# Largest key by products of whole key rows, a maximum along the free axis, and another planned order

## The chip, the cores and the metric

The kernel runs on one core of one Trainium2 chip. The metric is the device time of one execution in microseconds (us). The core has five engines that work side by side: TensorE (PE, whose weight loads are shown apart as PEld), VectorE (DVE), ScalarE (ACT), GpSimd (POOL) and SyncE (SP), which issues most DMAs. Each takes its instructions in the order in which the program gives them to it, and waits where an operand isn't there yet.

## The reference

Two branches over 2048 tokens of 448 features, and a gate for each token that mixes them. Branch A is attention with 16 heads of 28; branch B is a filter in the frequency domain.

```python
B, S, D = 1, 2048, 448
H = 16; Dh = D // H
g = sigmoid((x * gate_w).sum(-1, keepdims=True))
qkv = (x @ wqkv).reshape(B, S, 3, H, Dh).transpose(2, 0, 3, 1, 4)
q, k, v = qkv[0], qkv[1], qkv[2]
p = softmax(einsum("bhqd,bhkd->bhqk", q, k) * Dh ** -0.5)
a = (einsum("bhqk,bhkd->bhqd", p, v)).transpose(0, 2, 1, 3).reshape(B, S, D) @ wo
X = rfft2(x.astype(float32)) * (w_r + 1j * w_i)
b = irfft2(X, s=(S, D)).astype(bfloat16)
return g * a + (1 - g) * b
```

## The kernel before

The 16 heads are worked in four groups of four; the four heads of a group lie at partitions 0, 32, 64 and 96, 28 features each and a few rows for corrections. The queries go in 16 chunks of 512 tokens (four for each group), the keys in 16 tiles of 128. A score tile is keys by queries of one head, 128x512, a PSUM bank; there are 1024. Each is turned into exponentials in one of two ways: ACT computes them (line 1267, mostly two tiles in one instruction), or DVE writes an integer version that read as bf16 is about a power of two (line 1291), and POOL adds two shifted copies of up to three such tiles at once (line 1099). A tile that ACT made needs one product with the values V, a tile by way of DVE three.

All matrix products are issued by the helper at line 395, so they share this line, and are told apart by their tiles. `mc` splits a product by its columns of weights into strips of 32, at four positions of the array, which can run at the same time.

Scores are shifted by the largest squared norm of a key of the head, so that the exponentials stay in range. For group 0 this is done in units `kw0` with code of its own. For groups 1 to 3, POOL squares each chunk of keys (`e_ks`, line 732, into a free part of oT), and the unit `kw1`, `kw2` or `kw3` (function `largest`) works in six steps: `e_kx_pe` multiplies 16 tiles of squared keys with a selector of four columns, so that tokens lie on partitions and 64 sums on the free axis; `e_kx_m1` takes the maximum over the 16 tiles (128x4); `e_kx_tr` turns that round with the identity (4x128); `e_kx_mm` takes the maximum over 128; `e_kx_bc` spreads the four numbers over the heads' rows; `e_kx_kc` moves them to kc, which is added when q is moved out of PSUM (line 710). The q units of a group wait for its kw unit. The selector and the spreading matrix are columns 521 to 652 of the constant cA, which one DMA (`cA2`) brings.

The order of everything is set at build time by a planner written in Python (`Planner`, `stream`). It keeps a model clock for each engine, with durations written beside each step (`cols(n)` for a product of n columns, `dve(n)`, `act(n)`, or a number in us), and at each step places the piece of work that it can start first, ranked by due times. A unit's due time is a share of T plus an offset from the table OFF; some fifty parameters in PAR steer the choice between ACT and DVE, how early a unit may be taken and how many banks are kept. The engines then run the planned order whatever the real durations are.

The first 20 us prepare: x is loaded and transposed (units X0 to X7), folded on POOL for branch B (`e_xf`, lines 836 and 838, four pairs, xr and xe), the weights are loaded and spread to strips of 32 (line 474: `pk0` and `pq0` for group 0 on POOL, `pq1` and `pk1` for the other groups on DVE), and group 0's q and k are computed. The first fold waits for `pq0`, which waits for the load `wq0`. Small memsets on POOL behind the first pair (line 456) release later loads: the constants cC1 and cA2, and the weights wq1 and wk1 of the other groups, issued on SP's queue in this order.

Of the kernel before, what the change touches and what calls it, by code (L numbers as in the profile page):

```python
# [10 lines left out]
F32 = mybir.dt.float32  # L11
# [16 lines left out]
def fft_consts():  # L28
# [83 lines left out]
    A = np.zeros((128, 128 + 128 + 128 + 128 + 13 + 128))  # L112
    A[:, 0:128] = np.eye(128)
    for h in range(4):
        r = 32 * h
        A[r:r + 28, 128 + r + 28] = -0.5
        A[r:r + 28, 256 + r + 29] = -0.5
        A[r + 29, 512 + h] = 1.0
        A[r + 28:r + 32, 517 + h] = 1.0
        A[r:r + 28, 521 + h] = 1.0  # L120
        A[h, 525 + r + 29] = -0.5 * ALPHA
# [98 lines left out]
class Planner:  # L220
# [26 lines left out]
    def place(self, t, start):  # L247
        t.start = start
        t.end = start + t.dur
        if t.eng == "PE":  # L250
            if t.strips is None:
                self.strip = [t.end] * 4
                self.issue = t.end
            else:
                self.run_strips(t.strips, start + (0.0 if t.mode == self.mode else SW), True)
                t.end = max(self.strip)
        t.done = t.end + t.land
        t.placed = True
        self.free[t.eng] = t.end
        if t.mode is not None:  # L260
            self.mode = t.mode
        self.order.append(t)
        if t.then is not None:
            t.then(t)
# [34 lines left out]
class Kernel:  # L299

    PAR = dict(T=368, margin=0, dve_lead=1, pool_lead=8.025, early=156.198, dmargin=0, join=0.35, veff=0.55, vnext=0, vnb=2, nfa=6, nfd=1, flush=0.5, hold=4, n_dve=320, late=15.112, fill=0, cp=1.494, slack=0, zgap=0.3, vurg=24.651, nfa2=5, nfd2=0, trk=0.4, vrk=2.7, fitm=0.024, ukeep=3, dkeep=0, k3=4, w3=0, w2=0.055, amax=2, ulate=4, dsolo=0, k21=0, a21=0.7, qdn=15)


    OFF = dict(X0=-7.48, X1=-31.15, X2=-8.76, X3=-7.73, X4=10.34, X5=-2.42, X6=-12.59, X7=-5.72, q0_0=6.23, k0_0=13.58, k0_0b=13.14, k0_1=10.39,
               k0_2=-7.69, k0_3=19.38, kw0=3.44, v0_0=-126.42, v0_1=-47.49, v0_2=-26.74, v0_3=-11.95, q0_1=-18.46, q0_2=-3.0, q0_3=-2.59, gate=40.63,
               F1_0=12.99, F1_1=-23.99, F1_2=-34.12, F1_3=15.2, F1_4=7.02, F1_5=-8.21, F1_6=-1.1, F1_7=0.68, F1_8=6.09, F1_9=-43.2, F1_10=-34.66,
               F1_11=5.95, F1_12=8.95, F1_13=-13.79, F1_14=-3.63, F1_15=-17.27, k1_0=-15.54, k1_1=-1.12, k1_2=-6.24, kw1=-36.06, q1_0=7.64,
               v1_0=49.1, v1_1=49.43, v1_2=34.42, v1_3=-2.89, q1_1=-1.83, q1_2=23.85, q1_3=4.34, F2_0=-50.65, F3_0=55.06, F5_0=45.8, F2_1=-58.49,
               F3_1=-4.19, F5_1=31.73, F2_2=26.6, F3_2=6.07, F5_2=30.52, F2_3=-46.89, F3_3=37.68, F5_3=21.32, F2_4=-56.28, F3_4=7.86, F5_4=-1.49,
               F2_5=-19.46, F3_5=1.17, F5_5=45.52, F2_6=4.84, F3_6=1.14, F5_6=20.28, F2_7=9.15, F3_7=-17.95, F5_7=34.2, F2_8=27.09, F3_8=23.63,  # L310
               F5_8=57.9, F2_9=11.01, F3_9=11.74, F5_9=40.11, F2_10=3.19, F3_10=-20.19, F5_10=55.54, F2_11=-37.06, F3_11=50.1, F5_11=-45.25,
               F2_12=1.51, F3_12=-5.91, F5_12=37.08, F2_13=2.29, F3_13=-26.01, F5_13=7.42, F2_14=43.5, F3_14=25.25, F5_14=3.35, F2_15=-2.43,
               F3_15=33.4, F5_15=31.47, k2_0=-5.71, k2_1=-33.99, k2_2=-1.53, q2_0=-0.05, v2_0=8.32, v2_2=29.56, v2_3=15.17, q2_1=34.06, k3_0=-6.1,
               k3_1=14.07, k3_2=12.31, k3_3=-0.05, kw3=-8.76, q3_0=-29.03, v3_0=-4.47, v3_1=16.17, v3_2=11.35, v3_3=13.22, q3_1=0.16, q2_2=-2.51,
               q3_2=-24.22, q2_3=33.9, q3_3=-34.58, rg0=-0.08, rg1=-58.47, rg2=-25.93, rg3=-11.88, F6_0=1.79, F6_1=17.88, F6_2=1.0, F6_3=11.06,
               F6_4=50.13, F6_5=17.68, F6_6=60.78, F6_7=89.16, F6_8=61.03, F6_9=-9.62, F6_10=51.89, F6_11=-11.36, F6_12=5.82, F6_13=-35.13,
               F6_14=4.87, F6_15=35.02, o_1=5.5, o_2=28.97, o_3=-2.53, o_4=62.4, o_5=22.28, o_6=49.87, o_7=2.15, o_8=11.15, o_10=-22.91, o_11=21.75,
               o_12=-15.4, o_13=-16.58, o_14=17.26, o_15=-19.09)
# [15 lines left out]
    def sb(self, name, shape, dt=BF16):  # L334
        return self.per.tile(shape, dt, name=name)


    def tiles(self):
# [17 lines left out]
        self.cA = sb("cA", [128, 653])  # L356
# [21 lines left out]
        self.mx = sb("mx", [128, 1])  # L378
        self.kc = [sb(f"kc{i}", [128, 1], F32) for i in range(2)]
# [37 lines left out]
    def head(self):  # L417
# [18 lines left out]
        load("wq0", rawv[:, :, 0:112], wv[:, :, 0:112], 2.9, "ACT")  # L436
# [23 lines left out]
        load("cA2", self.cA[:, 521:653], C["A"].ap()[:, 521:653], 2.5, deps=[gate["cC1"]])  # L460
# [45 lines left out]
    def make_units(self):  # L506
# [4 lines left out]
        def unit(name, target, phases, deps=(), **k):  # L511
            u = U[name] = Unit(name, target + self.OFF.get(name, 0.0), phases, deps, **k)
            self.P.units.append(u)
            return u
# [7 lines left out]
        for k in range(4):  # L522
            dep[f"xr{k}"] = self.P.add("POOL", 1.84, lambda k=k: self.e_xf(k, 0), deps=[dep[f"x{k}"], dep["xrz"], dep["pq0"]], key=-5 if k == 0 else 0.5 * k)
            dep[f"xe{k}"] = self.P.add("POOL", 1.84, lambda k=k: self.e_xf(k, 1), key=-4.9 if k == 0 else 0.5 * k + 0.1,
                                       deps=[dep[f"xr{k}"], U[f"X{2 * k}"], U[f"X{2 * k + 1}"]])
# [56 lines left out]
        def largest(g, t0):  # L582

            unit(f"kw{g}", t0, [("PE", 0.43, self.e_kx_pe, (g,), "col"), ("DVE", 0.2, self.e_kx_m1, (g,)),
                                ("PE", 0.06, self.e_kx_tr, (g,), "col"), ("DVE", 0.25, self.e_kx_mm, (g,)),
                                ("PE", 0.04, self.e_kx_bc, (g,), "col"), ("DVE", 0.12, self.e_kx_kc, (g,))],
                 [dep[f"ks{g}_{c}"] for c in range(4)] + [dep["cA2"], dep["mxz"]], rank=-1)
# [146 lines left out]
    def e_kx_pe(self, b, g):  # L734
        for i in range(16):
            self.mc(b[:, 4 * i:4 * i + 4], self.oT[:, 3, 128 * i:128 * i + 128], self.cA[:, 521:525])

    def e_kx_m1(self, b, g):
        self.nc.vector.tensor_reduce(out=self.m1[:], in_=b[:, 0:64].rearrange("p (i h) -> p h i", h=4), axis=AX.X, op=ALU.max)

    def e_kx_tr(self, b, g):
        self.mm(b[0:4, 128:256], self.m1[:], self.ident, pos=(0, 0))

    def e_kx_mm(self, b, g):
        self.nc.vector.tensor_reduce(out=self.mx[0:4, :], in_=b[0:4, 128:256], axis=AX.X, op=ALU.max)

    def e_kx_bc(self, b, g):
        self.mc(b[:, 256:257], self.cA[:, 525:653], self.mx[:])
# [898 lines left out]
```

## Time and profile before

| what | us |
|---|---|
| median of 3 runs | 373.57 |
| lowest and highest of them | 373.29, 377.33 |
| the profiled execution | 373.71 |
| its span, first to last instruction | 371.9 |
| TensorE busy | 361.9 |
| ScalarE busy | 353.2 |
| VectorE busy | 325.6 |
| GpSimd busy | 320.1 |

A busy PE is one on which any product is under way; four strips at once count once. In a row of the timeline stand the start, the length, the engine, the line and the operation, the tiles out and in, the count of instructions merged, and in brackets the idle time of that engine before it with what ended it. In a row of the table by stage stand the stretch, and for each engine its busy time and number of instructions, then the mean granted TensorE clock (1.00 is full), the DMA share and GB/s. In a row of the chain of waits stand the start, the length and what ran.

### The profile page before, as it was taken

To read this page: it belongs to the slowest core of one execution; us is meant where nothing else is said; L and a number is where in the kernel's file an instruction comes from. 1 tells how busy PE (TensorE), PEld (TensorE's weight loads), DVE (VectorE), ACT (ScalarE), POOL (GpSimd) and SP (SyncE) were. 2 spreads that over 40 slices of the span, in tenths; PEclk is the share of its full clock that TensorE was granted. 3 is DMA by queue.
4 is the path that set the end of the run, shared out by engine and by line. 5 is a ranking of instruction groups with operands and counts; after the bars stand their busy time and mean duration, and the time that the engine had idled before them with its cause. 6 is when DMAs were issued, how large, how long until landed. Compare 5 with 4: busy or idle time off the path is not lost.

```text
span 371.9 us, 15399 instructions
## 1 busy us (share of the span) xinstructions
PE 361.9 (97%) x6712; PEld 140.9 (38%) x6712; DVE 325.6 (88%) x562; ACT 353.2 (95%) x403; POOL 320.1 (86%) x260
## 2 busy tenths in 40 slices
PE   8989999999999999999999999999999999999994
PEld 5434433333433334354433434343443333333332
DVE  4697899999988999899998879999999999998944
ACT  2879999999999999999999999999999999999991
POOL 7946799997899999888999979998799999999980
PEclk9989999999999999999999999999999999999999
DMA  8545410000100001232120000113000000000001
GB/s 258 123 104 89 113 45 2 4 4 2 30 3 3 18 16 30 56 84 73 42 57 3 18 2 4 42 39 89 17 14 26 5 14 14 14 14 26 27 3 63
DMA packets 18970, 14.78 MB, mean 40 GB/s; under 512 B 7924, under 2 KB 18518, under 8 KB 18903
## 3 DMA queue, kind: packets, MB, share of 16 engines
q1 hardware_dynamic: 17542, 13.00, 13.5%
q8 instruction: 52, 0.85, 1.0%
q10 hardware_dynamic: 1360, 0.81, 0.8%
q14 instruction: 16, 0.12, 0.1%
HBM read 11.96 MB, written 3.68 MB: 42 GB/s over the span
## 4 chain that ended last, share of the span: by engine, by line
PE 75%; ACT 12%; DVE 7%; issue 3%; POOL 2%; DMA 0%; DVEq 0%; ACTq 0%
PE bank L395 75%; ACT PA L1267 11%; DVE PD L1291 3%; POOL xr L836 2%; DVE AB L927 1%; POOL xt L838 1%; DVE xt L928 1%; DVE xt L929 1%; DMA out_dram<-fin 0%; DVE Z L914 0%; ACT fin L944 0%; PE bank L673 0%; DVE kT L712 0%; DVE xT L680 0%; DVE qT L710 0%
## 5 line engine op out<-in xcount | busy, mean ns | idle before, releaser
L1267 ACT ACTIVATE PA<-bank 128x1024 bf16<-128x1024 f32 (+1 forms) x379 | 338.4, 1105 | 1.7 <-PE bank L395 1.7
L1099 POOL TENSOR_SCALAR PD<-PD 128x1536 int16<-128x1536 int16 (+2 forms) x188 | 269.6, 1434 | 37.7 <-DVE PD L1291 24.1
L1291 DVE TENSOR_SCALAR PD<-bank 128x512 int16<-128x512 f32 x274 | 180.7, 683 | 18.1 <-PE bank L395 15.4
L395 PE MATMUL bank<-qT,kT 30*128 30x512 bf16 x1024 | 143.8, 385 | 1.0 <-ACT PA L1267 0.9
L395 PE MATMUL bank<-PA,V 128*32 128x512 bf16 x734 | 118.3, 383 | 0.0
L395 PE MATMUL bank<-PD,V 128*32 128x512 bf16 x822 | 118.1, 384 | 0.0
L395 PEld LDWEIGHTS <-kT 30*128 30x128 bf16 (+1 forms) x1040 | 38.5, 91 | 117.8 <-issue 113.2
L395 PEld LDWEIGHTS <-V 128*32 128x32 bf16 x1572 | 33.1, 95 | 42.5 <-issue 37.8
L395 PE MATMUL bank<-xT,Wp 112*32 112x512 bf16 (+3 forms) x528 | 40.3, 382 | 0.2
L395 PE MATMUL bank<-Wv,xT 112*32 112x112 bf16 (+1 forms) x1024 | 19.1, 214 | 0.0
L395 PE MATMUL bank<-Wo,oT 128*32 128x448 bf16 x256 | 17.6, 355 | 0.0
L897 DVE TENSOR_TENSOR TT<-bank,Wf 128x900 bf16<-128x900 f32 x16 | 17.0, 1085 | 0.3 <-issue 0.3
L395 PEld LDWEIGHTS <-xT 112*32 112x32 bf16 x1024 | 14.3, 96 | 6.7 <-issue 6.1
L395 PEld LDWEIGHTS <-Wp 112*32 112x32 bf16 (+1 forms) x528 | 9.9, 96 | 13.9 <-issue 12.3
L732 POOL TENSOR_TENSOR oT<-kT 128x512 bf16<-128x512 bf16 x12 | 12.4, 1040 | 0.5
L979 DVE TENSOR_TENSOR oT<-bank,oraw 128x512 bf16<-128x512 f32 (+1 forms) x19 | 11.2, 600 | 1.1 <-PE bank L395 1.1
L914 DVE CAST Z<-bank 113x512 bf16<-113x512 f32 x16 | 10.9, 686 | 0.7 <-PE bank L395 0.7
L697 DVE CAST sq<-bank 128x512 bf16<-128x512 f32 x15 | 10.2, 682 | 1.3 <-PE bank L395 1.3
L1267 ACT ACTIVATE oT<-bank 128x1024 bf16<-128x1024 f32 (+1 forms) x10 | 8.3, 861 | 2.9 <-PE bank L395 2.9
L712 DVE CAST kT<-bank 128x512 bf16<-128x512 f32 x15 | 10.2, 681 | 0.9 <-PE bank L395 0.9
L884 DVE CAST AB<-bank 128x448 bf16<-128x448 f32 x16 | 9.9, 619 | 1.2 <-PE bank L395 1.1
L699 DVE TENSOR_TENSOR sq<-bank,sq 128x512 bf16<-128x512 f32 x15 | 10.4, 691 | 0.5
(91 smaller groups left out, 284.9 us busy)
## 6 DMA issues: line engine op xcount, KB each, us to landing
cM<-cM SPq DMA_DIRECT2D x16, 128.0 KB, 3.5
cG<-cG SPq DMA_DIRECT2D x16, 128.0 KB, 2.7
Wf<-Wd SPq DMA_DIRECT2D x32, 56.2 KB, 2.2
out_dram<-fin SPq DMA_DIRECT2D x15, 112.0 KB, 1.7
xt<-in_A_x_dram SPq DMA_DIRECT2D x2, 448.0 KB, 5.0
Z<-in_A_wqkv_dram SPq DMA_DIRECT2D x2, 294.0 KB, 3.8
Wd<-in_B_w_r_dram SPq DMA_DIRECT2D x4, 112.5 KB
Wd<-in_B_w_i_dram SPq DMA_DIRECT2D x4, 112.5 KB, 6.1
```

Source lines behind the costliest of these rows:

```text
L395: self.nc.tensor.matmul(out, lhsT=lhsT, rhs=rhs, start=start, stop=stop, skip_group_check=True, **k)
L697: self.nc.vector.tensor_copy(out=t, in_=b)
L699: self.nc.vector.tensor_tensor(out=t, in0=b, in1=t, op=ALU.mult)
L712: self.nc.vector.tensor_copy(out=self.kT[g % 2][:, 512 * c:512 * c + 512], in_=b)
L732: self.nc.gpsimd.tensor_tensor(out=self.oT[:, 3, 512 * c:512 * c + 512], in0=k, in1=k, op=ALU.mult)
L884: self.nc.vector.tensor_copy(out=self.AB[bg % 2][:, 0:448], in_=b[:, 0:448])
L897: self.nc.vector.tensor_tensor(out=self.TT[bg % 2][:].rearrange("p w r f -> p w (r f)").rearrange("p w (r f) -> p w r f", r=2), in0=bc_at( ...
L914: self.nc.vector.tensor_copy(out=self.Z[:, :, :, :, 8 * bg:8 * bg + 8].rearrange("p c t s e -> p c (t s) e"), in_=b[0:113, :].rearrange("p ...
L979: nc.vector.tensor_tensor(out=self.oT[:, g, 512 * c + c0:512 * c + c1], in0=b[:, c0:c1], in1=oraw[:, c0:c1], op=ALU.mult)
L1099: nc.gpsimd.tensor_scalar(out=t[:, j, 0:n, :], in0=t[:, 0, 0:n, :], scalar1=float(sh), scalar2=1.0, op0=ALU.add, op1=ALU.mult)
L1267: nc.scalar.activation(out=buf, in_=src, func=ACT.Exp, scale=LN2 / 128.0)
L1291: nc.vector.tensor_scalar(out=dst, in0=self.bank[b], scalar1=C2, scalar2=0.0, op0=ALU.add, op1=ALU.max)
```

## The change

The six steps of `largest` become seven. The selector, now 32 columns wide with 28 zero columns, is the weight, and the squared keys, 512 tokens at a time, are what moves: four products at four strips put the sums of head h of token chunk c at partition 32c + h, with the 512 tokens along the free axis. One maximum over the bank gives 128 numbers (`mc1`). A product with a mask (`e_kx_sp`) spreads them to 128x4, one column for each chunk, `e_kx_tr` gathers rows h, 32 + h, 64 + h and 96 + h to row h, and `e_kx_mm` takes the maximum over four.

The planner's costs change in four places: the steps of kw, 1.94 instead of 1.84 for each of the eight folds, 3.6 instead of 2.9 for the landing of wq0, and 0.01 on the strips when the array changes to products by strips. All of PAR and nearly all of OFF have other values (one row of PAR and the first of OFF shown).

```diff
-    A = np.zeros((128, 128 + 128 + 128 + 128 + 13 + 128))
+    A = np.zeros((128, 128 + 128 + 128 + 128 + 41 + 136))
...
-        A[h, 525 + r + 29] = -0.5 * ALPHA
+        A[h, 553 + r + 29] = -0.5 * ALPHA
+        A[h::32, 681 + h] = 1.0
+        A[r:r + 32, 685 + h] = 1.0
...
                 t.end = max(self.strip)
+                if t.mode == "col" and t.mode != self.mode:
+                    self.strip = [x + 0.01 for x in self.strip]
...
-    PAR = dict(T=368, margin=0, dve_lead=1, pool_lead=8.025, early=156.198, dmargin=0, join=0.35, veff=0.55, vnext=0, vnb=2, nfa=6, nfd=1, flush=0.5, hold=4, n_dve=320, late=15.112, fill=0, cp=1.494, slack=0, zgap=0.3, vurg=24.651, nfa2=5, nfd2=0, trk=0.4, vrk=2.7, fitm=0.024, ukeep=3, dkeep=0, k3=4, w3=0, w2=0.055, amax=2, ulate=4, dsolo=0, k21=0, a21=0.7, qdn=15)
+    PAR = dict(T=368, margin=0, dve_lead=1.065, pool_lead=10.679, early=374.528, dmargin=0.3, join=0.1, veff=0.9, vnext=4, vnb=3, nfa=2, nfd=2, flush=0.2, hold=4, n_dve=380.349, late=8, fill=1, cp=1.617, slack=0.884, zgap=0.6, vurg=24.799, nfa2=5, nfd2=0, trk=0.361, vrk=2.7, fitm=0.02, ukeep=3, dkeep=0, k3=2, w3=0.3, w2=0.091, amax=2, ulate=16.42, dsolo=0, k21=0, a21=1, qdn=15)
...
-    OFF = dict(X0=-7.48, X1=-31.15, X2=-8.76, X3=-7.73, X4=10.34, X5=-2.42, X6=-12.59, X7=-5.72, q0_0=6.23, k0_0=13.58, k0_0b=13.14, k0_1=10.39,
+    OFF = dict(X0=5.19, X1=-27.98, X3=0.84, X5=5.45, X6=-20.0, q0_0=-17.13, k0_0=0.4, k0_0b=14.3, k0_1=31.05, k0_2=-0.87, k0_3=24.59, v0_0=-34.41,
...
-        self.cA = sb("cA", [128, 653])
+        self.cA = sb("cA", [128, 689])
...
+        self.mc1 = sb("mc1", [128, 1], F32)
...
-        load("wq0", rawv[:, :, 0:112], wv[:, :, 0:112], 2.9, "ACT")
+        load("wq0", rawv[:, :, 0:112], wv[:, :, 0:112], 3.6, "ACT")
...
-        load("cA2", self.cA[:, 521:653], C["A"].ap()[:, 521:653], 2.5, deps=[gate["cC1"]])
+        load("cA2", self.cA[:, 521:689], C["A"].ap()[:, 521:689], 2.5, deps=[gate["cC1"]])
...
-            dep[f"xr{k}"] = self.P.add("POOL", 1.84, lambda k=k: self.e_xf(k, 0), deps=[dep[f"x{k}"], dep["xrz"], dep["pq0"]], key=-5 if k == 0 else 0.5 * k)
-            dep[f"xe{k}"] = self.P.add("POOL", 1.84, lambda k=k: self.e_xf(k, 1), key=-4.9 if k == 0 else 0.5 * k + 0.1,
+            dep[f"xr{k}"] = self.P.add("POOL", 1.94, lambda k=k: self.e_xf(k, 0), deps=[dep[f"x{k}"], dep["xrz"], dep["pq0"]], key=-5 if k == 0 else 0.5 * k)
+            dep[f"xe{k}"] = self.P.add("POOL", 1.94, lambda k=k: self.e_xf(k, 1), key=-4.9 if k == 0 else 0.5 * k + 0.1,
...
-            unit(f"kw{g}", t0, [("PE", 0.43, self.e_kx_pe, (g,), "col"), ("DVE", 0.2, self.e_kx_m1, (g,)),
-                                ("PE", 0.06, self.e_kx_tr, (g,), "col"), ("DVE", 0.25, self.e_kx_mm, (g,)),
+            unit(f"kw{g}", t0, [("PE", cols(512), self.e_kx_pe, (g,), "col"), ("DVE", 0.62, self.e_kx_m1, (g,)),
+                                ("DVE", 0.1, self.e_kx_sp, (g,)), ("PE", 0.03, self.e_kx_tr, (g,), "col"), ("DVE", 0.25, self.e_kx_mm, (g,)),
...
     def e_kx_pe(self, b, g):
-        for i in range(16):
-            self.mc(b[:, 4 * i:4 * i + 4], self.oT[:, 3, 128 * i:128 * i + 128], self.cA[:, 521:525])
+
+        for c in range(4):
+            self.mm(b[32 * c:32 * c + 32, :], self.cA[:, 521:553], self.oT[:, 3, 512 * c:512 * c + 512], pos=(0, 32 * c))
 
     def e_kx_m1(self, b, g):
-        self.nc.vector.tensor_reduce(out=self.m1[:], in_=b[:, 0:64].rearrange("p (i h) -> p h i", h=4), axis=AX.X, op=ALU.max)
+        self.nc.vector.tensor_reduce(out=self.mc1[:], in_=b, axis=AX.X, op=ALU.max)
+
+    def e_kx_sp(self, b, g):
+        self.nc.vector.tensor_scalar(out=self.m1[:], in0=self.cA[:, 685:689], scalar1=self.mc1[:, 0:1], scalar2=None, op0=ALU.mult)
 
     def e_kx_tr(self, b, g):
-        self.mm(b[0:4, 128:256], self.m1[:], self.ident, pos=(0, 0))
+        self.mm(b[0:4, 0:4], self.cA[:, 681:685], self.m1[:], pos=(0, 0))
 
     def e_kx_mm(self, b, g):
-        self.nc.vector.tensor_reduce(out=self.mx[0:4, :], in_=b[0:4, 128:256], axis=AX.X, op=ALU.max)
+        self.nc.vector.tensor_reduce(out=self.mx[0:4, :], in_=b[0:4, 0:4], axis=AX.X, op=ALU.max)
 
     def e_kx_bc(self, b, g):
-        self.mc(b[:, 256:257], self.cA[:, 525:653], self.mx[:])
+        self.mc(b[:, 256:257], self.cA[:, 553:681], self.mx[:])
```

## What I predict

> **What bounds the kernel now.** I read the page first: span, busy shares, the chain by engine.
>
> ```profile
> span 371.9 us, 15399 instructions
> PE 361.9 (97%) x6712; PEld 140.9 (38%) x6712; DVE 325.6 (88%) x562; ACT 353.2 (95%) x403; POOL 320.1 (86%) x260
> PE 75%; ACT 12%; DVE 7%; issue 3%; POOL 2%; DMA 0%; DVEq 0%; ACTq 0%
> ```
>
> TensorE and ScalarE are both nearly full, and the table by stage says where they are not (columns: PE, weight loads, DVE, ACT, POOL busy; clock; DMA):
>
> ```profile
> 10.00:20.00 10.00, 8.37 (x131) 4.11 (x131) 6.73 (x9) 7.61 (x12) 9.84 (x10) 0.97 0.49 115
> 20.00:30.00 10.00, 9.76 (x184) 4.14 (x181) 9.10 (x18) 8.60 (x11) 5.02 (x5) 0.86 0.54 107
> 60.00:100.00 40.00, 39.98 (x827) 15.53 (x828) 37.72 (x65) 40.00 (x46) 34.78 (x25) 1.00 0.04 9
> 260.00:300.00 40.00, 39.61 (x651) 14.66 (x651) 38.80 (x74) 39.61 (x45) 35.21 (x29) 1.00 0.05 15
> ```
>
> Between 60 and 100 us, and nearly so up to 300, there is no hole on either engine, so a gain comes from fewer PE microseconds there, or from the first 30 us, where ACT lacks 3.8 us in two rows and the granted clock is below 1. The chain in order of time (start, length, what) says the same: PE carries 31 to 185 us without a break, and before that a fold of POOL and one hole lead to it.
>
> ```profile
> 16.43 1.89 POOL xt L838
> 18.32 1.05 issue
> 19.37 3.52 PE bank L395 x37
> 31.18 40.98 PE bank L395 x817
> 72.19 112.98 PE bank L395 x2290
> 213.41 2.54 ACT PA L1267 x3
> ```
>
> The timeline shows the hole (start, length, engine, what, idle before it); the last three rows are the table by stage again, cut finer:
>
> ```profile
> 6.15 0.56 POOL L474 COPY Wp<-Z 112x448 bf16<-112x448 bf16 x1 [0.70 <-DMA Z<-in_A_wqkv_dram]
> 10.56 0.13 POOL L456 MEMSET Z<- 1x1 bf16 x2
> 11.04 1.04 SPq L405 DMA_DIRECT2D cA<-cA  x1
> 16.51 2.16 DVE L474 COPY Wp<-Z 112x1344 bf16<-112x1344 bf16 x1 [1.48 <-DMA Z<-in_A_wqkv_dram]
> 18.59 0.68 DVE L712 CAST kT<-bank 128x512 bf16<-128x512 f32 x1
> 19.34 0.15 PEld L395 LDWEIGHTS <-xt 128*32 128x32 bf16 x8 [1.97 <-issue]
> 20.52 1.51 ACT L1267 ACTIVATE oT<-bank 128x1024 bf16<-128x1024 f32 x2 [1.89 <-PE bank L395]
> 22.91 1.94 ACT L1267 ACTIVATE PA<-bank 128x1024 bf16<-128x1024 f32 x2 [0.88 <-PE bank L395]
> 17.79:19.34 1.55, 0.00 (x0) 0.00 (x0) 1.55 (x3) 0.84 (x2) 1.55 (x2) 1.00 0.14 39
> 19.50:20.00 0.50, 0.50 (x19) 0.27 (x11) 0.50 (x1) 0.00 (x0) 0.50 (x1) 0.50 0.52 144
> 22.50:23.00 0.50, 0.50 (x6) 0.14 (x8) 0.50 (x2) 0.09 (x1) 0.50 (x2) 0.62 0.50 75
> ```
>
> In its order, DVE stood 1.48 us waiting for the later heads' weights (a DMA that POOL's small memset at 10.56 releases), then copied them for 2.16 us, and only then moved the first whole chunk of k to kT, ending at 19.27; PE resumes 0.07 us later. The trace books the gap as issue; the two times make kT's move its cause, more than the fold that ended at 18.32. PE did nothing for 1.55 us. Then the granted clock was 0.5, until about 22.9 by its mean of 0.62 in the last row, so of some 3.4 us another 1.7 were lost. ACT lost 1.89 + 0.88 = 2.77 us.
>
> **The change part by part.** The span is 371.9; its run took 373.71, so 1.8 lie around it. The median is 373.57, 0.14 less. I sum against 373.71.
>
> First, the products. Rows of the first group:
>
> ```profile
> 68.51 0.64 PE L395 MATMUL bank<-cA,oT 128*32 128x4 bf16 x64
> 69.00 0.62 PE L395 MATMUL bank<-PD,V 128*32 128x512 bf16 x8
> 69.55 0.39 PE L395 MATMUL bank<-qT,kT 30*128 30x512 bf16 x3
> 69.26 0.22 DVE L739 TENSOR_REDUCE m<-bank 128x4 bf16<-128x64 f32 x1
> 70.62 0.27 DVE L745 TENSOR_REDUCE mx<-bank 4x1 bf16<-4x128 f32 x1
> 131.47 0.64 PE L395 MATMUL bank<-cA,oT 128*32 128x4 bf16 x64
> 214.60 0.64 PE L395 MATMUL bank<-cA,oT 128*32 128x4 bf16 x64
> 217.93 0.15 DVE L751 COPY kc<-bank 128x1 f32<-128x1 f32 x1
> 223.68 0.66 DVE L710 TENSOR_SCALAR qT<-bank,kc 128x512 bf16<-128x512 f32 x1
> ```
>
> The 64 products of 4 columns hold PE from 68.51 to 69.00, 0.49 us. Four products of 512 columns, one on each strip of 32, are what a block of four PV products is; two such blocks take 0.62 and one product lasts 0.39, so a block adds 0.23. Saving: 0.26 a group. The second group, at 131.5, also lies in PE's part of the chain. The third, at 214.6, stands where the chain runs over ACT (from 213.41 on); I count it at nothing. The product of m1 has 4 columns instead of 128 on one strip, beside PV products on the others: nothing to 0.05. Together 2 x 0.26 = 0.5 us of PE on the path (bounds 0 to 0.9).
>
> DVE: the maximum over 512 f32 in PSUM instead of 64. From 64 to 128 elements the rows rise by 0.05, so 512 give 0.22 + 7 x 0.05 = 0.57; moving 512 elements out of PSUM took 0.68 (kT above). I take 0.65, +0.43. The new masking of 128x4 is nearest to the kc copy, 0.15. The maximum over 4 instead of 128 falls from 0.27 to between 0.15 and 0.22, say -0.1. Net +0.5 a group, 1.5 in all. DVE has 2.3 us free between 60 and 100, so work there covers it. Behind it stand DVE's own exponentials, by at most 0.65 us in one place. Who waits for the whole: the next q chunk of that group, and in the last group, where it follows soonest, it is moved at 223.7, 5.6 us after kc is there at 218.1. With the cover gone it would be PE waiting 0.5 a group, +1.5 at most. I take 0.
>
> The second constants' DMA grows from 132 to 168 columns, 33 to 42 KB, and goes ahead of the later heads' weights on SP's queue; its issue took 1.04 us, so by proportion 0 to 0.28 later weights; I take 0.1, in the head below. The tile mc1, the shifted columns of cA and the 0.01 us that the planner adds on a change of mode have no instruction of their own: zero.
>
> Second, the planner's costs at the head. Folds go from 1.84 to 1.94, the first q weights' landing from 2.9 to 3.6:
>
> ```profile
> L836 POOL TENSOR_TENSOR xr<-xt 128x896 bf16<-128x896 bf16 x4 | 7.8, 1942 | 0.0
> L474 DVE COPY Wp<-Z 112x1344 bf16<-112x1344 bf16 x2 | 3.7, 1871 | 1.5 <-DMA Z<-in_A_wqkv_dram 1.5
> ```
>
> Nothing gets faster by that; the order is laid out for later times. Two folds stand ahead of the memset that releases the weights: 0.7 (the wait at 6.15 is 0.70) + 2 x 0.1 = 0.9 us of lateness is now in the plan. So other DVE work should stand ahead of the copy, and the wait of 1.48 shrinks to 0.6, with the larger DMA 0.7. The copies are still planned at 0.75 and take 1.87 on average, so an overrun of 1.1 each stays. PE's gap then goes from 1.55 to about 0.75. A shorter pause in PE left the clock whole, 0.70 us out of these six:
>
> ```profile
> 210.00:216.00 6.00, 5.30 (x190) 2.79 (x186) 4.57 (x9) 5.94 (x7) 5.76 (x6) 1.00 0.10 25
> ```
>
> That sum may hide two pauses, but none of it lowered the clock, and 0.75 is nearer to that row than to the 1.55 that halved it, and I take the clock as whole: PE gains 0.8 + 1.7 = 2.5, ACT 0.8 + 0.88 = 1.7. Bounds: 0, if the new order puts the copy where it was, and PE 3.25 with ACT 2.77 if the hole goes entirely; below nothing by one more such hole, 3.25.
>
> The Trainium skill, TensorE: Matmul & The Clock Gate (Part 1: The HAM clock gate), says that the clock falls to half after an idle window of about 3.4 us that runs freely. By it 1.55 us of nothing should not suffice; this trace has the half clock right behind 1.55 us. If it is the rule that holds, the low clock came from more than the gap.
>
> Third, PAR and OFF: a new order of every stage, with the same arithmetic. Its scale is the trade between ACT and PE:
>
> ```profile
> 349.49 13.10 ACT L1267 ACTIVATE PA<-bank 128x1024 bf16<-128x1024 f32 x15
> L1291 DVE TENSOR_SCALAR PD<-bank 128x512 int16<-128x512 f32 x274 | 180.7, 683 | 18.1 <-PE bank L395 15.4
> L395 PE MATMUL bank<-PD,V 128*32 128x512 bf16 x822 | 118.1, 384 | 0.0
> 361.92 0.40 DVE L927 CAST AB<-bank 128x225 bf16<-128x225 f32 x1 [4.58 <-PE bank L395]
> ```
>
> A score tile on ACT costs 13.10 / 30 = 0.44 us; on DVE it costs PE three PV products instead of one (822 is 3 x 274), 2 x 0.23 / 4 = 0.12 us. PE has 0.5 + 2.5 = 3.0 to give, ACT 1.7: x tiles moved from ACT to DVE gain 1.7 + 0.44x = 3.0 - 0.12x, x = 2.3, 2.7 us; an order that moves none gains 1.7. I take 2.3. The tail (two last fold-backs at 361.9 behind an idle DVE, then outputs to 371.9) may change by 1 us either way; I take 0.
>
> Sum: 373.71 - 2.3 = 371.4, less 0.14 for the median: 371.2.
>
> **The rivals.**
> 1. *The head stays slow.* The copy's overrun of 1.1 us each is uncorrected, and if the half clock has another cause than the gap, a shorter gap doesn't lift it. PE gains 0.5 + 0.8 = 1.3 and ACT 0.8 at best, nothing but the products at worst: 0.5 to 0.9, so 372.9. For it: the copy is unchanged in the diff. Against it: the clock is whole up to the hole. By the Trainium skill's rule (TensorE: Matmul & The Clock Gate, Part 1: The HAM clock gate), read strictly, it is this case that comes.
> 2. *The hole goes entirely.* PE 0.5 + 3.25 = 3.75, ACT 2.77: 2.77 + 0.44x = 3.75 - 0.12x, x = 1.75, 3.5 us; with 0.7 us from the tail 369.4. For it: every target of the head changes, so the copy may stand behind k's chunks. Against it: PE's later work needs those chunks anyway, and a hole of 0.3 may remain.
> 3. *Slower: one more hole.* The new order lets PE wait once for DVE for 1.5 us or more, with the clock halved behind it, 3.25 each; DVE, busy 38.80 of 40 between 260 and 300 and now with 1.5 us more, is where it would start. One on top of the old hole gives 373.57 - 0.5 + 3.25 = 376.3; it is slower than before from a loss of 0.5 on. Against it: in the trace of before DVE's 97% there cost PE only 0.4 us.
> 4. *No difference.* The order before was also laid out against the same model, and everything but the products cancels: 373.1; it lies within the first rival's range and counts with it.
>
> **How the numbers follow.** Forecast (371.2) 0.42; rivals 1 and 4 together (372.9) 0.22; rival 2 (369.4) 0.24; rival 3 (376.3) 0.12. One per cent, about what a measurement of this kernel can tell from no change, is 3.7 us: 369.8 and 377.3. Faster by more: most of rival 2 and the lower edge of the forecast, 0.26. Slower by more: two thirds of rival 3, if it strikes harder than once, 0.08. Within: 0.66. The forecast's own range is 370.2 to 372.4; the wide one leaves out the better half of rival 2 and most of rival 3: 368.6 to 374.8.
>
> **What would show it.** Right: 12 products of 512 columns in place of 192 of 4; a maximum of 0.57 to 0.69 and three maskings of 0.15; DVE's wait before the first wide copy near 0.7 and PE's gap behind it under 1 us, with the clock at 1.0 from there to 30 us; ACT over 9.5 of 10 between 20 and 30; a DVE count of tiles a few above 274. Wrong: a clock of 0.5 in the first 30 us behind a gap under 1 us (rival 1), or a gap of 1.5 us or more anywhere later (rival 3). If the head is mended as said and the time isn't near 371, the order of the middle or the tail has given it back.

## The result, and the profile after

| | median us | range | executions |
|---|---|---|---|
| before | 373.58 | 370.67 to 379.02 | 20 |
| after | 375.66 | 374.89 to 377.56 | 20 |

The ratio is 1.0077, with a 95% interval of 1.0057 to 1.0098: 0.8% slower, some 2.9 us, where 371.2 and a range up to 374.8 were predicted. In some executions, all of them of kernels with the order of before and the wide copies as planned, the chip granted a mean clock of 0.970 to 0.986 and the time was some 1.5% longer; the ratios here leave these out and the medians don't, so differences to before are read from the ratios (0.1% is 0.37 us). The means of all 20 executions, 374.65 and 375.84, lie 1.2 us apart. The profiled execution of after took 376.95 us, with a span of 375.2.

The page of after, busy time by engine and the chain that ended last by engine:

```profile
PE 363.3 (97%) x6526; PEld 140.4 (37%) x6526; DVE 327.9 (87%) x564; ACT 355.2 (95%) x411; POOL 319.6 (85%) x262
PE 59%; ACT 22%; DVE 12%; issue 4%; DMA 1%; POOL 1%; DVEq 0%; SPq 0%; ACTq 0%
```

PE has 186 instructions fewer and yet 1.4 us more busy time; more of its work ran at a lower clock, as the stages below show. ACT has 2.0 us more, its share of the chain rose from 12 to 22%, and DVE's from 7 to 12%. Where PE and ACT lose time, the stages of after tell (in each stretch the busy time of PE, PEld, DVE, ACT and POOL, then the clock, the DMA share and GB/s):

```profile
10.00:20.00 10.00, 8.53 (x131) 3.86 (x129) 6.51 (x8) 9.10 (x14) 9.84 (x10) 1.00 0.56 126
20.00:30.00 10.00, 8.37 (x164) 4.49 (x168) 8.18 (x18) 6.91 (x10) 5.01 (x5) 0.67 0.60 113
30.00:40.00 10.00, 10.00 (x265) 4.92 (x261) 6.46 (x12) 8.47 (x12) 4.80 (x5) 0.82 0.40 79
100.00:140.00 40.00, 39.15 (x704) 14.47 (x700) 34.90 (x58) 39.39 (x48) 37.29 (x31) 1.00 0.07 20
180.00:220.00 40.00, 39.99 (x846) 16.48 (x842) 35.56 (x58) 40.00 (x47) 35.91 (x31) 1.00 0.13 36
220.00:260.00 40.00, 39.16 (x711) 14.43 (x708) 37.61 (x62) 39.40 (x46) 33.75 (x29) 1.00 0.09 25
260.00:300.00 40.00, 38.90 (x632) 14.49 (x629) 37.57 (x75) 39.67 (x48) 35.15 (x28) 1.00 0.04 11
```

The same view of before, for three stretches that the prediction didn't show:

```profile
100.00:140.00 40.00, 40.00 (x770) 14.44 (x765) 35.51 (x61) 40.00 (x47) 38.00 (x30) 1.00 0.03 9
180.00:220.00 40.00, 39.25 (x760) 15.13 (x757) 34.80 (x58) 39.58 (x45) 38.00 (x30) 1.00 0.09 25
220.00:260.00 40.00, 40.00 (x763) 15.66 (x763) 37.41 (x60) 40.00 (x47) 35.25 (x31) 1.00 0.16 40
```

There are three places. Between 20 and 40 ACT lost 1.7 and 1.5 us against before, at a lower clock; as it had done 1.5 us more between 10 and 20, about half of this is a real loss. In 100 to 140 and 220 to 260 PE, which had no idle time before, lost 0.85 and 0.84. In 260 to 300 it lost 0.7. The other way, 180 to 220 is full in after and lacked 0.75 in before. The PE waits of after, in total, times and longest:

```profile
PE bank L400 <- DVE kT L717: 2.1, 1, 2.1
PE bank L400 <- DVE m L748: 1.5, 2, 0.8
```

The first is the head, the second the new mask. The timeline of after at the head (start, duration, operation, and in brackets the idle time before it with what ended it):

```profile
16.13 1.88 POOL L847 TENSOR_TENSOR xt<-xt 128x896 bf16<-128x896 bf16 x1
16.88 3.60 DVE L479 COPY Wp<-Z 112x1344 bf16<-112x1344 bf16 x2 [0.41 <-DMA Z<-in_A_wqkv_dram]
17.96 2.14 POOL L845 TENSOR_TENSOR xr<-xt 128x896 bf16<-128x896 bf16 x1
20.19 2.04 POOL L847 TENSOR_TENSOR xt<-xt 128x896 bf16<-128x896 bf16 x1
20.40 1.27 DVE L717 CAST kT<-bank 128x512 bf16<-128x512 f32 x2
21.13 0.39 PE L400 MATMUL bank<-qT,kT 30*128 30x512 bf16 x3 [2.07 <-DVE kT L717]
21.56 1.02 ACT L1276 ACTIVATE PA<-bank 128x1024 bf16<-128x1024 f32 x1 [1.87 <-PE bank L400]
```

DVE's wait ahead of the first wide copy did shrink, from 1.48 to 0.41. But the two copies now stand back to back, and the two k chunks for which PE waits stand behind both. Read their ends against POOL's: the fold begun at 16.13 ends at 18.01, the next at 20.10, and the second copy ends at 20.48, 0.38 after that. In before, by the rows of the prediction, the first copy ended at 18.67, 0.35 after the fold of 16.43 and 1.89 us. So it looks as if a wide copy does 0.35 to 0.38 us of work after POOL's running instruction has ended, and the rest is waiting for that end; a_late below tests it. The reverse shows too: a fold that began while a copy held on took 2.14 or 2.04, not 1.88.

PE's gap is 2.07 us where 1.55 stood, and behind it the clock is half for 10.2 us (the same view of stretches, by hand-picked bounds):

```profile
20.00:23.40 3.40, 1.76 (x27) 0.97 (x27) 3.33 (x8) 1.84 (x3) 2.93 (x3) 1.00 0.64 131
23.40:33.60 10.20, 10.20 (x221) 5.36 (x217) 6.86 (x15) 7.45 (x10) 3.41 (x4) 0.50 0.60 98
33.60:37.00 3.40, 3.40 (x107) 1.82 (x108) 3.01 (x6) 3.10 (x5) 1.13 (x2) 0.99 0.09 13
```

The mask, in the timeline of after around its second group:

```profile
134.28 0.40 PE L400 MATMUL bank<-oT,cA 128*32 128x512 bf16 x4
134.29 3.02 POOL L1108 TENSOR_SCALAR PD<-PD 128x1536 int16<-128x1536 int16 x2
135.53 0.68 DVE L745 TENSOR_REDUCE mc<-bank 128x1 f32<-128x512 f32 x1
136.25 1.08 DVE L748 TENSOR_SCALAR m<-cA,mc 128x4 bf16<-128x4 bf16 x1
137.38 0.17 PE L400 MATMUL bank<-m,cA 128*4 128x4 bf16 x1 [0.76 <-DVE m L748]
```

The mask has four columns and takes 1.08 us. It ends at 137.33 (136.25 + 1.08), and POOL's pair of instructions at 137.31 (134.29 + 3.02). The product that needs it waits 0.76. The maximum just ahead of it, which reads PSUM, ran its 0.68 beside the same POOL work undisturbed. By tile (least, median and most in ns), the three masks of after are

```profile
L748 DVE TENSOR_SCALAR m<-cA,mc x3: 319/977/1081, 73.9 to 226.6; 128x4 bf16<-128x4 bf16 x3
```

### The profile page after: what moved, and what is told of

It is laid out like the page before. It is cut to its first block, busy times and chain, and to the rows that moved or that the text cites. A ratio compares the mean times of both kernels' runs of the same rounds, so it can differ in the third digit from the quotient of the medians.

```text
span 375.2 us, 15055 instructions
## 1 busy us (share of the span) xinstructions
PE 363.3 (97%) x6526; PEld 140.4 (37%) x6526; DVE 327.9 (87%) x564; ACT 355.2 (95%) x411; POOL 319.6 (85%) x262
## 4 chain that ended last, share of the span: by engine, by line
PE 59%; ACT 22%; DVE 12%; issue 4%; DMA 1%; POOL 1%; DVEq 0%; SPq 0%; ACTq 0%
PE bank L400 58%; ACT PA L1276 22%; DVE PD L1300 5%; PE bank L678 1%; DMA Z<-in_A_wqkv_dram 1%; DVE AB L936 1%; DVE xt L938 1%; DVE sq L704 1%; DVE xt L937 1%; DVE sq L702 1%; DVE m L748 1%; DVE kT L717 0%; DVE mc L745 0%; DVE oraw L969 0%; POOL xr L845 0%
## 5 line engine op out<-in xcount | busy, mean ns | idle before, releaser
L400 PE MATMUL bank<-PD,V 128*32 128x512 bf16 x819 | 120.4, 383 | 0.0
L400 PE MATMUL bank<-Wv,xT 112*32 112x112 bf16 (+1 forms) x1024 | 19.9, 225 | 0.1
L400 PE MATMUL bank<-Wo,oT 128*32 128x448 bf16 x256 | 18.6, 356 | 0.3 <-DVE oT L988 0.3
L400 PEld LDWEIGHTS <-xT 112*32 112x32 bf16 x1024 | 15.3, 102 | 6.6 <-issue 6.1
L913 POOL TENSOR_TENSOR TT<-TT 128x225 bf16<-128x225 bf16 x16 | 9.0, 562 | 3.4 <-DVE TT L906 2.8
L856 DVE CAST U__76<-bank 113x512 bf16<-113x512 f32 x16 | 10.6, 680 | 0.5 <-PE bank L400 0.5
L702 DVE CAST sq<-bank 128x512 bf16<-128x512 f32 x15 | 10.2, 681 | 0.5 <-PE bank L400 0.5
```

Source lines behind the costliest of these rows:

```text
L400: self.nc.tensor.matmul(out, lhsT=lhsT, rhs=rhs, start=start, stop=stop, skip_group_check=True, **k)
L702: self.nc.vector.tensor_copy(out=t, in_=b)
L856: self.nc.vector.tensor_copy(out=o, in_=b[0:113, :].rearrange("p (c g e) -> p c g e", c=4, g=16))
```

## The experiments

Two theories came out of this. *P*: the mask and the wide copies, DVE instructions that read and write SBUF alone, are held until POOL's running instruction ends, and PE waits for the mask. *H*: the hole at the head (two copies held by folds ahead of two k chunks, PE idle, the clock halved) costs the change more than it cost before. Against them stood the possibilities that the new steps are dear by themselves, that the new order is worse as a whole, and that the half clock comes without the gap. The kernels with a_ keep the change's planned order, those with b_ the order of before. All the results, with the ratio to before run beside them:

| kernel | order | largest-key steps | copies | median us | ratio (95%) |
|---|---|---|---|---|---|
| after_again | after | new | as planned | 375.80 | 1.0098 (1.0071 to 1.0126) |
| a_mask | after | new, mask from PSUM | as planned | 374.59 | 1.0064 (1.0039 to 1.0090) |
| a_late | after | new | later | 372.85 | 1.0027 (1.0000 to 1.0054) |
| a_oldkx | after | old | as planned | 374.80 | 1.0079 (1.0048 to 1.0110) |
| a_both | after | new, mask from PSUM | later | 371.64 | 0.9989 (0.9965 to 1.0012) |
| a_warm | after | new | as planned, zero products | 374.84 | 1.0053 (1.0023 to 1.0083) |
| b_late | before | old | later | 370.29 | 0.9946 (0.9895 to 0.9997) |
| b_late_again | before | old | later | 370.81 | 0.9959 (0.9919 to 1.0000) |
| b_newkx | before | new | as planned | 376.26 | 1.0075 (1.0039 to 1.0111) |
| b_newkx_mask | before | new, mask from PSUM | as planned | 373.87 | 0.9995 (0.9962 to 1.0028) |
| b_all | before | new, mask from PSUM | later | 371.51 | 0.9985 (0.9952 to 1.0018) |
| b_all_tr | before | as b_all, mask's product later | later | 371.14 | 0.9971 (0.9935 to 1.0006) |

**The change once more, beside the first experiments**, as the value that they are compared with.

> The changed kernel once more, as the base for the runs beside it. From its first result 375.66 us, 0.6 to 1.0% slower than before. Every theory expects the same; the gap of PE near 19 us and the half clock behind it should be there again if they belong to the order and not to one execution.

It took 375.80, and the loss stands: 3.6 us by its ratio, 2.9 by the first one. PE's gap is there again (1.94 us), and so is the half clock (a mean of 0.56 from 20 to 30 us).

**a_mask: the mask reads PSUM.** One operand of the mask comes from the bank of the products. The larger of mc1 and one of the values of which mc1 is the maximum is mc1 again, so what is computed doesn't change.

```diff
-        self.nc.vector.tensor_scalar(out=self.m1[:], in0=self.cA[:, 685:689], scalar1=self.mc1[:, 0:1], scalar2=None, op0=ALU.mult)
+        self.nc.vector.scalar_tensor_tensor(out=self.m1[:], in0=b[:, 0:4], scalar=self.mc1[:, 0:1], in1=self.cA[:, 685:689],
+                                            op0=ALU.max, op1=ALU.mult)
```

> The changed kernel with one instruction of another form: the mask reads the bank of sums in PSUM as its first operand (maximum with mc1, which leaves mc1, then times the mask), in the same order. Theory P (the mask is held up by POOL's running instruction, because both its operands lie in SBUF): the three masks fall from 0.32, 1.08 and 0.98 us to at most 0.25, PE's two waits for them (0.76 and 0.72) go, and the time falls by 0.5 to 1.5, to about 374.6. Rival (the mask is slow by itself, or waits for the maximum just before it): it stays over 0.3 and the time stays at 375.7. Rival O (the new order's length sets the time, and these waits are covered): the mask gets short and the time stays within 0.4 of 375.7.

By tile, and by stage in a_mask:

```profile
L748 DVE SCALAR_TENSOR_TENSOR m<-bank,mc,cA x3: 222/223/223, 73.3 to 225.3; 128x4 bf16<-128x4 f32 x3
```

```profile
100.00:140.00 40.00, 39.91 (x721) 14.81 (x718) 34.82 (x60) 40.00 (x49) 37.90 (x32) 1.00 0.07 18
220.00:260.00 40.00, 39.99 (x730) 14.82 (x727) 37.71 (x63) 40.00 (x46) 34.37 (x30) 1.00 0.09 23
```

Three masks of 0.22, none drawn out, and PE's idle time in both stretches is gone. The time fell by 1.2 us. Theory P held. The edit changes two things at once, the instruction and the place of one operand, so which of them frees it from POOL isn't told apart here; the maximum ahead of it, which also reads PSUM, wasn't held either.

**a_late: the two wide copies moved back in DVE's order**, behind the k chunks and the first group's kw steps.

```diff
-        for t in self.P.order:
+        o = self.P.order
+        for name, at in (("pk1", 174), ("pq1", 199)):
+            t = self.dep[name]
+            o.remove(t)
+            o.insert(at, t)
+        for t in o:
             t.fn()
```

> The changed kernel with the two wide copies of weights moved later in DVE's order, behind the moves of group 0's k chunks and before their first use; nothing else moves. Theory H (the hole at the head and the half clock behind it are what makes the change slower): PE's gap falls from 2.07 to under 0.5 us, the clock is 1.0 from 20 to 40 us, ACT loses less than 1 us there instead of 5, and the time falls by 2 to 4.5, to about 372.5. Rival C (the half clock has another cause than the gap): the gap goes, the clock still shows 0.5 somewhere in the first 40 us, and the time falls by 1 or less. Rival O (order of the rest): the head mends, and the time stays near 375.

The timeline of a_late, and three stretches of it:

```profile
19.15 1.29 DVE L722 CAST kT<-bank 128x512 bf16<-128x512 f32 x2 [1.74 <-PE bank L400]
19.62 0.67 PE L400 MATMUL bank<-qT,kT 30*128 30x512 bf16 x4
20.63 1.89 POOL L852 TENSOR_TENSOR xt<-xt 128x896 bf16<-128x896 bf16 x1
...
21.81 0.40 PE L400 MATMUL bank<-sq,cA 128*32 128x512 bf16 x4 [0.50 <-DVE sq L709]
...
23.64 0.18 PE L400 MATMUL bank<-mn,cA 4*128 4x1 bf16 x2 [0.33 <-DVE mn L786]
...
24.84 0.49 DVE L484 COPY Wp<-Z 112x1344 bf16<-112x1344 bf16 x1
28.00 0.50 DVE L484 COPY Wp<-Z 112x1344 bf16<-112x1344 bf16 x1
```

```profile
20.00:24.00 4.00, 3.16 (x55) 1.64 (x51) 3.93 (x9) 3.96 (x6) 3.23 (x3) 1.00 0.55 122
24.00:27.50 3.50, 3.50 (x106) 2.46 (x103) 2.64 (x7) 3.17 (x5) 2.27 (x2) 0.51 0.53 100
27.50:31.00 3.50, 3.50 (x114) 1.79 (x114) 3.49 (x9) 3.01 (x5) 1.14 (x2) 1.00 0.59 106
```

Each copy took 0.49 or 0.50 us, starting after the last fold; scores follow the k chunks at once, and the time fell by 2.95 us. Of the 3.60, all but some 1.0 was thus POOL's doing. Of the rival on the clock a part held as well: one stretch of 3.5 us at half clock came with no longer wait of PE in the 4 us ahead of it than 0.50.

**a_oldkx: the order of the change with the old largest-key steps** (of the edit, the products and the mask; the maxima and the turn go back in the same way).

```diff
-        for c in range(4):
-            self.mm(b[32 * c:32 * c + 32, :], self.cA[:, 521:553], self.oT[:, 3, 512 * c:512 * c + 512], pos=(0, 32 * c))
+        for i in range(16):
+            self.mc(b[:, 4 * i:4 * i + 4], self.oT[:, 3, 128 * i:128 * i + 128], self.cA[:, 521:525])
...
     def e_kx_sp(self, b, g):
-        self.nc.vector.tensor_scalar(out=self.m1[:], in0=self.cA[:, 685:689], scalar1=self.mc1[:, 0:1], scalar2=None, op0=ALU.mult)
+        pass
```

> The changed kernel's order with the former steps of the largest key: 64 products of 4 columns, a maximum over 16, the turn with the identity, a maximum over 128; nothing stands in the mask's place. Theory P (the new steps cost PE two waits of 0.76 and 0.72 us, more than the 0.5 us of products that they save): 0.5 to 1.2 faster than the changed kernel, about 374.8. As the prediction had it (the products save 0.5 and the rest is hidden): 0.5 slower, 376.2. Rival O: within 0.3 of the changed kernel.

It is 1.0 us faster than the change by the medians (0.7 by the ratios, whose intervals overlap): in the very order planned for them, the new steps gain nothing and probably lose.

**a_both: a_mask and a_late together.**

> The changed kernel with both: the mask that reads PSUM and the two wide copies moved later. If the two causes add (1.2 us for the mask and 2.9 for the copies in the runs just made), 371.7, and not slower than the kernel before beside it; if one covers the other, 372.8. The masks take 0.22, PE waits for none of them, and PE has no gap over 0.7 us in the first 60 us.

371.64: the two add up (375.80 - 1.21 - 2.95 = 371.64). The head isn't whole even so: in its profiled execution the clock was half from about 22.6 to 29.4, though PE's longest wait in the 4.6 us ahead of it was 0.50.

**a_warm: eight products of zeros in PE's gap**, into a bank that the scores behind it overwrite. They are work beyond the computation and keep PE busy.

```diff
-        for t in self.P.order:
+        for i, t in enumerate(self.P.order):
+            if i == 136:
+                v = dict(zip(t.fn.__code__.co_freevars, (c.cell_contents for c in t.fn.__closure__)))
+                for k in range(8):
+                    self.mm(self.bank[v["sets"][0][1]], self.zz[:, 0:128], self.zz)
             t.fn()
```

> The changed kernel with eight products of zeros put into PE's gap near 19 us, written to the bank that the waiting scores overwrite; DVE's order, the wait for kT and all else stay. It parts the gap from the clock. Theory W (the clock falls where PE does too little in a stretch, and the gap is what made it too little): the scores still start only when kT is there, near 21 us, but the clock stays at 1.0 for at least 3 us longer or wholly, and the time falls by 1.0 to 2.5, to about 374. Rival (the clock falls whatever fills the gap): the half clock is there as before, 8 to 10 us long, and the time stays at 375.7.

The timeline (which has seven of the eight products) and the stages of a_warm:

```profile
20.36 1.90 PE L400 MATMUL bank<-zz 128*128 128x512 bf16 x7
22.19 0.39 PE L400 MATMUL bank<-qT,kT 30*128 30x512 bf16 x3
```

```profile
20.00:30.00 10.00, 9.25 (x200) 4.72 (x201) 9.70 (x19) 8.34 (x12) 5.93 (x5) 1.00 0.57 115
30.00:40.00 10.00, 9.72 (x294) 4.80 (x282) 7.69 (x16) 9.90 (x15) 6.32 (x7) 1.00 0.39 80
```

The scores start no earlier, but the clock is whole. That alone gave 1.0 us by the medians and 1.7 by the ratios; that the rest of a_late's 2.95 is the lateness itself is argued, not shown.

**b_late: the copies late in the order of before** (the edit of a_late, with 172 and 211).

> The kernel before with its two wide copies moved later in the same way; all else is the kernel before. Theory H: its gap of 1.55 us and the half clock of 3.4 us go in most executions; PE and ACT both lose less, and it is 1 to 2 us faster than the kernel before beside it, about 371. Rival (in this order the gap is covered, since only ACT's 2.77 us count and they come back later): within 0.5 of the kernel before.

The gap is gone, but in the profiled execution the clock still went to half:

```profile
20.00:30.00 10.00, 9.47 (x165) 4.30 (x165) 7.71 (x17) 8.74 (x12) 4.79 (x5) 0.71 0.57 107
30.00:40.00 10.00, 10.00 (x243) 4.66 (x235) 6.37 (x14) 8.23 (x10) 5.45 (x5) 0.77 0.38 62
```

Cut finer, it was 0.50 from 24.3 to 34.5, and PE's longest wait in the 6 us ahead of it was 0.23. In b_late_again the clock was whole from 20 to 40.

> The order of before with the two wide copies moved back, nothing else, beside the run with both mends on the same chip: 370.3 us again, ratio 0.993 to 0.996. The difference to the run with both mends is what the new largest-key steps are worth once their mask is cheap and the hole at the head is gone: theory P says 0 to 0.5 us in their favour, rival N 1 us or more against them.

0.9946, and 0.9959 beside the last experiments: 1.5 to 2.0 us faster than before (the intervals reach from 0 to 3.9), with the lowest medians of all. So moving the copies was worth 1.5 to 2.0 us in before, and 2.6 to 2.95 in after, where the change was to have closed the hole.

**b_newkx and b_newkx_mask: the new steps in the order of before**, each mask right behind its maximum, once as in the change and once from PSUM.

> The order of the kernel before with the new steps of the largest key put in place of the old, the mask right behind the maximum. It is the change's first part alone. As the prediction had it (two groups' products save 0.26 us each, DVE's 0.5 a group is hidden): 0.5 faster. Theory P (each mask waits for POOL's running instruction, up to 1.5 us, and PE's next product of the group waits behind it): one to three masks take 0.3 to 1.5 us, PE waits, and it is 0.3 to 1.5 slower than the kernel before beside it.

> The order of before, with the new largest-key steps right behind one another, and with the mask's first operand in PSUM. Theory P (the mask is dear only because it reads and writes SBUF while POOL works): each mask takes 0.22 us as it did in the order of the change, PE waits for it no more than 0.3 us each, and the products' saving of 2 x 0.26 us stays: 372.5 to 373.5 us, ratio 0.997 to 1.001, against 1.0075 with the mask in SBUF. Rival N (the new steps are dear on their own, by the maximum over 512 that is 0.4 us longer, three times): the time stays 1.0 us or more above before, ratio 1.003 or more.

By tile and by PE's waits in b_newkx:

```profile
L747 DVE TENSOR_SCALAR m<-cA,mc x3: 230/815/1310, 72.5 to 220.4; 128x4 bf16<-128x4 bf16 x3
```

```profile
PE bank L398 <- DVE m L747: 3.2, 3, 1.4
```

Without any new order the new steps cost 2.8 us by the ratio, more than P's 1.5, and PE waits 3.2 us for the mask; with the mask from PSUM they cost nothing (0.9995). In its direction theory P held. But PE still waits 1.6 us for that mask, up to 0.64 at a time where 0.3 was expected: it stands behind a maximum of 0.68. And the new steps gain nothing, where 0.5 us of saved products were to remain.

**b_all and b_all_tr: both mends in the order of before**, and then the mask's product moved back on PE.

```diff
+        for g in (1, 2, 3):
+            ts = [t for t in o if t.unit is not None and t.unit.name == f"kw{g}"]
+            tr, mm = ts[-4], ts[-3]
...
+            o.remove(tr)
+            o.insert(o.index(mm), tr)
```

> The order of before with both mends: the mask's first operand in PSUM and the two wide copies moved back in DVE's order. If the two parts add up (the copies were worth 2.9 us in the order of before, the new steps with the cheap mask 0 to 0.5 us), 369.8 to 370.4 us, ratio 0.990 to 0.995, and it is the fastest of all. If the order of the change were the better one apart from its two faults, this would be no faster than that order with both mends, which took 371.64 us.

The PE waits and the timeline of b_all:

```profile
PE bank L398 <- DVE m L752: 1.6, 3, 0.6
```

```profile
129.18 0.68 DVE L748 TENSOR_REDUCE mc<-bank 128x1 f32<-128x512 f32 x1
129.90 0.22 DVE L752 SCALAR_TENSOR_TENSOR m<-bank,mc,cA 128x4 bf16<-128x4 f32 x1
130.17 0.16 PE L398 MATMUL bank<-m,cA 128*4 128x4 bf16 x1 [0.57 <-DVE m L752]
```

0.26 us of products are saved in a group, and then PE, which works in order, stands 0.36 to 0.64 us for a maximum and a mask of 0.90 where a maximum of 0.22 was planned. b_all is 0.7 us behind b_late_again by the medians and 1.0 by the ratios, within their intervals; the parts didn't add up here. The 2.9 us that the expectation counts for the copies is by the medians; by the ratios it is 1.5 to 2.0.

> The order of before with both mends, and the product of the mask moved back on PE in the three later groups, past the two or three blocks of products that stood between it and the maximum behind it. With both mends alone PE still waited for the mask 1.6 us in three times (0.36, 0.57 and 0.64), because the order of before counts 0.2 us for a maximum that now takes 0.68 and a mask of 0.22. Theory W (the saved products are handed back in this wait): the waits fall below 0.3 us together, the time from 371.51 to 370.0 to 371.0 us, ratio 0.991 to 0.997. Rival E (PE has slack there, and the end is set by ACT and DVE): the waits go and the time stays at 371.2 to 371.8.

In the list of PE's waits of b_all_tr the mask is gone, and the small maximum behind it came instead:

```profile
PE bank L398 <- DVE mx L765: 0.5, 2, 0.3
```

The 1.6 us are now 0.5. The time fell by 0.4, less than W said and with an interval that spans it, and stayed behind b_late. The waits explain a part; whether the rest is noise or ACT's bound isn't settled.

## Why the prediction was wrong

**The products: right in size, wrong in what they bring.** Twelve products of 512 stand in place of 192 of 4; the four of a group run side by side and end 0.40 us after their start, one product's length (0.39 in the prediction's row). PE's busy time is 0.57 us less in b_all than in b_late_again (359.77 against 360.34, the stages summed). Nothing of it that can be measured reached the end: with the cheap mask the new steps are 0.2 us ahead of the old ones in the order of after (a_mask, a_oldkx), level in that of before (0.9995), and 0.7 behind with the copies late (b_all, b_late_again), all differences of at most 0.3%, which the intervals span.

**The mask at 0.15 and "I take 0": this step failed first.** The price was taken from the row "it is nearest to", the kc copy. But that copy reads PSUM, and the mask reads and writes SBUF while POOL works. The masks took 0.32, 1.08 and 0.98; PE waited 1.5 us. The bound, "PE waiting 0.5 a group, +1.5 at most", named the right waiter, PE behind DVE, and I put it aside because DVE has free time in that stage. A mean of free time over 40 us covers no wait in one place. That its sum came out is luck: it was three times 0.5 of added DVE work, and what came was two waits of 0.76 and 0.72 for a mask that POOL held. Worth: 1.2 us in the order of the change.

The Trainium skill states the mechanism (SBUF — State Buffer, "Who interferes with whom"): VectorE and GpSimd share a pair of SBUF ports by an exclusive lock held for a whole instruction, which copies and tensor_scalar in a fast mode need and a reduction never does. The traces agree, row by row: the mask ends with POOL's instruction (137.33 beside 137.31) and the wide copies 0.35 to 0.38 after it, the maximum doesn't wait (0.68), and the mask that reads PSUM takes 0.22.

**The wide copies' overrun of 1.1 "stays": right. The gap of 0.75: wrong.** "Other DVE work should stand ahead of the copy" came true for one k chunk, and the wait shrank to 0.41, even more than the 0.7 predicted. But I let the gap shrink by as much as the wait shrank. Two copies back to back, each held by a fold, put 3.60 us between one k chunk and the next, and the gap grew to 2.07. I had read the 1.87 in the view of groups as the copy's price, and not asked what makes a copy of 0.5 that long; its end beside POOL's would have told.

**The clock "as whole": wrong.** It was half for 10.2 us in the profiled execution of after. a_warm prices it at 1.0 to 1.7 us. That it follows from the gap alone, as I took it, doesn't hold: a_late, a_both and b_late have it without one. The gap makes it likelier. The mean clock stayed below 0.995 in all 20 executions of after, in 2 of 11 of a_warm, 1 of 12 of a_late, 6 of 12 of a_both and 2 of 8 of b_late. So a part of the first rival's condition, another cause than the gap, held. The head, entered at a gain of 1.7 to 2.5, gave none and costs after about 1 us more than before; of the whole miss of 4.5 us (375.66 against 371.2) this is the largest part.

**More tiles on DVE: wrong in direction.** The rows of the page for ACT's exponentials and DVE's tiles in after:

```profile
L1276 ACT ACTIVATE PA<-bank 128x1024 bf16<-128x1024 f32 (+1 forms) x386 | 340.4, 1088 | 7.1 <-PE bank L400 6.6
L1300 DVE TENSOR_SCALAR PD<-bank 128x512 int16<-128x512 f32 x273 | 180.1, 682 | 16.7 <-PE bank L400 14.6
```

DVE has 273 tiles, one fewer, not "a few above 274", and ACT's come in 386 instructions where before had 379:

```profile
L1267 ACT ACTIVATE PA<-bank 128x1024 bf16<-128x1024 f32 (+1 forms) x379 | 338.4, 1105 | 1.7 <-PE bank L395 1.7
```

That is 2.0 us more on ACT: one tile (0.44), and, split by form, 37 instructions on single tiles where 24 stood; that these make up the rest is argued, not shown. ACT's idle time ahead of them, nearly all of it waiting for PE, rose from 1.7 to 7.1, which is more. The 0.6 us of this trade were a guess at what a plan would do, not a reading of a row.

**The rivals.** The third rival's mechanism came, at other places: PE waits for DVE for the mask and at the head, with the half clock behind the latter. Its place, 260 to 300, did lose 0.7 us of PE's time; it lost as much in a_both (38.86 of 40), which is no slower than b_all, so no cost is shown for it. That rival's time, 376.3, is near 375.66 by luck, as the loss is made up of other parts than one hole of 3.25; its chance of 0.12 was too low all the same: a change that adds three DVE steps to a chain on which PE waits in order deserved more.

**The sum.** By the ratios, against before: the mask 1.2 (after_again against a_mask); the head 0.6 to 1.4 (2.6 to 2.95 in after, 1.5 to 2.0 in before); what is left with both mended, 1.1 to 1.6 (a_both, 0.4 below before, against 1.5 to 2.0 below it for b_late). Together 2.9 to 4.2, for a measured 2.9 to 3.6; as the parts are steps along one row of kernels they must about add up, so this is no test of them. Of the last part, about 1.0 may be the new steps with a cheap mask (b_all against b_late_again, though a_mask against a_oldkx has them ahead by 0.2) and the rest the order; intervals of 0.3% either way, 1.2 us, don't separate them, and this part stays open.

## What to carry to other kernels

Price an added DVE instruction by where its operands lie and what POOL does at that time, not by its size: one that stays within SBUF can last until POOL's instruction ends, and one operand from PSUM mended that here. Work saved on an engine that runs in order is handed back at the next thing it waits for; when a step of another engine in between gets longer, the consumer has to move too. Before an order is planned anew, look at the durations that the trace contradicts: the copies, planned at 0.75, take 0.49 where POOL stands idle and up to 2.16 beside a fold, and the planner put both beside folds. No run here planned with other durations.

## What the runs showed of the hardware that was not expected

A mask of 128x4 lasted from 0.23 to 1.31 us, a wide copy from 0.49 to over 2, by what POOL was doing; the same size with an operand in PSUM lasted 0.22 each time.

The half clock came in stretches of 3.4 (before), 3.5 (a_late), 6.8 (a_both), 10.2 (after, b_late) and 13.7 us (b_newkx), about one to four times 3.4. In before and after it stood behind gaps of 1.55 and 2.07, in a_late where PE had just waited 0.50 and 0.33 us in 20 to 24, and in b_late where it had waited no more than 0.23 at a time. While it lasted PE was busy throughout (10.20 of 10.20 us in after and in b_late), so that busy time alone did not end it. The Trainium skill (TensorE: Matmul & The Clock Gate, "Part 1: The HAM clock gate") tells of free-running windows of about 3.4 us; the length of the stretches agrees, but no gap here filled a window. Zero products in the gap kept the clock whole in the profiled execution of a_warm, so that PE's idleness takes part in it. What exactly sets it off stays open: a_late and b_late show that a long gap isn't needed.
